# Half-height scores for the first batch, one spread row in place of two, and a new order of the opening

## The chip, the cores and the metric

The kernel runs on one core of one Trainium2 chip. The metric is the device time of one execution in microseconds; the figure for a kernel is the median of its runs. A profiled execution is told beside it, with its own time.

The core has a matrix engine (PE, with its weight loads shown apart as PEld), a vector engine (DVE), an engine for activations and copies (ACT), a general engine (POOL) and an engine that mostly issues transfers (SP). Each takes its instructions in the order of the program. Transfers (DMA) are issued by SP, ACT and POOL into queues that share 16 DMA engines.

## The reference

Eight batches of eight heads; 576 rows of 64 numbers for each head in q, k and v. Keys and values are averaged over groups of 8 rows, so that 72 pooled keys stand for 576. Then a mixing layer over the rows and a two-layer network follow. Cut to what matters:

```python
k_p = k.reshape(B, H, Sp, 8, D).mean(axis=3)          # 72 pooled keys
v_p = v.reshape(B, H, Sp, 8, D).mean(axis=3)
attn = softmax(q @ k_p.T / 8)                          # 576 x 72
x = (attn @ v_p) as (B, 576, 512)                      # heads side by side
tok = einsum('ts,bsd->btd', w_tok, alpha1 * x + beta1)
u = x + lam * tok
out = u + lam * (relu((alpha2 * u + beta2) @ w_ch1) @ w_ch2)
```

## The kernel before

The work is cut into batches (attention) and into blocks of four chunks of 128 rows (mixing and network). The order of all instructions is written out by hand. From the second batch on, attention runs inside the network's work: a list of (due time, step) pairs is sorted and issued. For the first batch there is nothing to hide it in: the code issues it as a plain sequence at the end of the kernel's body, from `keep_warm(13)` to the loop `for j in range(4): mlp_A(0, j, 256, 512)`. That sequence is called the opening here, and it is what the change touches.

The steps of the opening, with the lines of their main instructions:

- `att_F(0, hp)` (L402, copy L409): four transposes of q on PE for a pair of heads, then a copy into `qT`. `att_Frem` (L426, L429): the same for the last 64 rows of all heads, after `cast_rem` (L170).
- `double_k(u)` (L433, and L178, L179 for u = 0) and `att_K(0, u)` (L445, L451): the pooled keys of four heads by 20 small products. The result has the two halves of the row pairs on partitions 0 to 63 and 64 to 127.
- In `att_K`, for the first batch, two copies (L461) put each half into a tile `kpT` whose other half is zero. So `att_S(0, h)` can run each product over all 128 rows: three products for a head (256 columns, 256 columns and 64 columns; L493, L496), and two exponentials on ACT (L498). For later batches `att_K` makes one copy (L457) and `att_S4` runs products over 64 rows each (L513, L520).
- `first_V(0, u)` (L472 over 128 rows, L474 over 32 rows, copy L477): the pooled values of four heads.
- `att_AV(0, h)` (L556, L560, then L562 and L564 on DVE): the weighted values of one head. `att_X` and `rest_X` (L578, L571) multiply by lambda times alpha1, mostly on POOL.
- `spread_lam` (L304, L305) spreads the row lambda over 128 partitions by two passes of a one-row product and a copy on ACT; `spread_al1(half)` (L311, L312) does the same with one half of alpha1 and multiplies by lambda on DVE.
- `setup_wtok` (L329, L332) and `setup_rowsum` (L341, L343) prepare the mixing matrix; `mix_T(0, c)` (L614, then L618, and L624 with `al2_bc` on POOL or DVE) mixes; `mix_uT` (L638, L640) transposes; `mlp_A` (L662, L669) is the first layer of the network.
- `keep_warm(n)` (L605): n products of 512 columns whose result nobody reads.
- `load_al2` (L298, L299): a one-column memset on DVE, and behind it SP's transfer of alpha2, spread over 128 partitions by the transfer itself.

Products write into eight PSUM banks: six taken in turn by `gp`, two by the tag `ch`.

## Time and profile before

| | |
|---|---|
| median of 3 runs | 334.22 us (333.26 to 334.68) |
| the profiled execution | 333.62 us, of which the span of instructions is 331.9 us |
| PE busy | 323.7 us (98%) |
| DVE, ACT, POOL busy | 233.6, 175.7, 95.2 us |
| mean granted PE clock | 0.995 |
| chain that ended last | PE 94%, DMA 2%, DVE 1%, issue 1%, POOL 1% |

How to read it: times inside the execution are counted from the start of the span. The products of PE overlap each other, and their ends are modelled; the spacing of their starts is the firmer number, and it is what is used below. An engine's idle time has a releaser: the instruction whose end let it go on. The chain of waits starts at the last instruction and goes back, at each step to what released it, or to the instruction before it on its engine.

### The profile page before, as it was taken

Reading aid. Unit: us, or ns where it says so; the run is one execution under the profiler, and the core shown is the slowest. Engines: PE = TensorE matmul, PEld = TensorE weight load, DVE = VectorE, ACT = ScalarE, POOL = GpSimd, SP = SyncE. Lnnn points to the kernel's source line nnn. Section 1 sums busy time; section 2 is a strip of 40 time slices with the busy share of each in tenths; the row PEclk is TensorE's granted clock in tenths of the full one; section 3 lists DMA queues with packets and bytes.
Section 4 is the critical chain, followed back from the end, with each engine's and each line's share of the span. In section 5 each row is a group of like instructions: output and inputs, shape, how many; then the busy total and the mean of one; then the engine's idle time right before and its main releaser. Section 6 shows DMA issues by size and latency. Waiting matters only on the chain.

```text
span 331.9 us, 6477 instructions
## 1 busy us (share of the span) xinstructions
PE 323.7 (98%) x2500; PEld 209.6 (63%) x2531; DVE 233.6 (70%) x485; ACT 175.7 (53%) x322; POOL 95.2 (29%) x110
## 2 busy tenths in 40 slices
PE   7999999999999999999999999999999999999995
PEld 3667864455544576656775677558755866586584
DVE  6674289989679969676967796877788783263263
ACT  3584989448422861388128812682268225703710
POOL 8669828401247011800280027102510200000000
PEclk9799999999999999999999999999999999999999
DMA  8999999966895992499449943996340044004003
GB/s 117 191 217 270 270 209 245 206 148 101 152 243 99 219 181 81 80 232 173 147 109 209 173 136 73 209 187 176 65 136 2 0 65 143 2 0 127 1 32 97
DMA packets 66472, 45.81 MB, mean 138 GB/s; under 512 B 34397, under 2 KB 57061, under 8 KB 66442
## 3 DMA queue, kind: packets, MB, share of 16 engines
q1 hardware_dynamic: 52092, 32.67, 43.3%
q0 software_dynamic: 13824, 12.40, 22.9%
q8 instruction: 20, 0.33, 0.4%
q10 hardware_dynamic: 526, 0.34, 0.4%
q14 instruction: 10, 0.08, 0.1%
HBM read 38.30 MB, written 9.44 MB: 144 GB/s over the span
## 4 chain that ended last, share of the span: by engine, by line
PE 94%; DMA 2%; DVE 1%; issue 1%; POOL 1%; ACT 0%; POOLq 0%
PE ps_h L662 38%; PE ps_w L785 26%; PE ps_tok L614 11%; PE ps_ch L682 8%; PE ps_av L556 3%; PE ps_s L513 2%; DMA k<-in_k_dram 2%; PE ps_kp L445 1%; PE ps_sc L493 1%; PE ps_r L520 1%; PE ps_av L560 1%; PE ps_v L472 0%; PE ps_w L329 0%; PE ps_q L402 0%; DVE u_sb L618 0%
## 5 line engine op out<-in xcount | busy, mean ns | idle before, releaser
L662 PE MATMUL ps_h<-u_fm,w 128*128 128x512 bf16 (+2 forms) x588 | 132.6, 368 | 1.3 <-DVE bias_cols L665 0.2
L669 ACT ACTIVATE H<-ps_h,bias_cols 128x512 bf16<-128x512 f32 x144 | 98.2, 688 | 56.5 <-PE ps_h L662 55.5
L662 PEld LDWEIGHTS <-w 128*128 128x128 bf16 x608 | 65.6, 114 | 49.9 <-issue 2.2
L785 PEld LDWEIGHTS <-H 128*128 128x128 bf16 x560 | 53.5, 98 | 10.8 <-DVE u_sb L803 1.2
L622 ACT CAST u_bf<-u_sb 128x512 bf16<-128x512 f32 x32 | 19.8, 618 | 69.9 <-issue 39.9
L785 PE MATMUL ps_w<-w_l,H 128*128 128x256 bf16 x448 | 53.6, 272 | 0.0
L803 DVE TENSOR_TENSOR u_sb<-u_sb,ps_w 128x512 f32<-128x512 f32 x54 | 36.3, 683 | 17.1 <-PE ps_w L785 17.1
L578 POOL TENSOR_TENSOR xs<-x_tm,lamal_bc 128x512 bf16<-128x512 f32 x12 | 15.9, 1328 | 108.7 <-DVE x_tm L564 108.5
L614 PE MATMUL ps_tok<-xs,wtT 128*128 128x512 bf16 (+3 forms) x194 | 44.6, 380 | 0.4
L618 DVE TENSOR_TENSOR u_sb<-x_tm,ps_tok 128x512 f32<-128x512 f32 (+1 forms) x40 | 27.4, 684 | 9.9 <-PE ps_tok L614 9.8
L564 DVE TENSOR_TENSOR x_tm<-ps_av,rec 128x320 f32<-128x320 f32 x64 | 31.5, 492 | 2.6
L542 ACT ACTIVATE ET<-ps_s 72x512 f16<-72x512 f32 x56 | 32.3, 592 | 0.0
L614 PEld LDWEIGHTS <-wtT 128*128 128x128 bf16 (+3 forms) x200 | 17.4, 100 | 16.0 <-issue 1.1
L562 DVE RECIPROCAL rec<-ps_av 128x5 f32<-128x5 f32 x64 | 12.2, 190 | 16.9 <-PE ps_av L560 16.7
L483 DVE TENSOR_TENSOR v_u<-v_u 72x1024 f32<-72x1024 f32 (+1 forms) x24 | 22.7, 948 | 0.2
L785 PE MATMUL ps_w<-w_t,h_s 128*128 128x256 bf16 x168 | 22.6, 272 | 0.0
L682 PEld LDWEIGHTS <-H 128*128 128x128 bf16 x128 | 11.9, 98 | 13.7 <-issue 0.4
L754 DVE TENSOR_TENSOR H<-H,H 128x1024 bf16<-128x1024 bf16 x14 | 9.7, 690 | 14.3 <-ACT H L669 14.2
L185 POOL TENSOR_TENSOR k_raw<-k_raw 128x512 f32<-128x512 f32 x14 | 18.8, 1341 | 0.9 <-PE ps_ch L682 0.7
L785 PEld LDWEIGHTS <-h_s 128*128 128x128 bf16 x168 | 16.4, 98 | 4.1
L187 POOL TENSOR_TENSOR k_bf<-k_raw 128x512 bf16<-128x512 f32 x14 | 18.5, 1319 | 1.1
L754 DVE TENSOR_TENSOR h_s<-H 128x1024 bf16<-128x1024 bf16 x21 | 14.4, 686 | 6.0 <-ACT H L669 5.8
(148 smaller groups left out, 367.6 us busy)
## 6 DMA issues: line engine op xcount, KB each, us to landing
out_dram<-u_sb SPq DMA_DIRECT2D x29, 256.0 KB
k_raw<-in_k_dram SPq DMA_DIRECT2D x12, 512.0 KB
v_u<-in_v_dram SPq DMA_DIRECT2D x12, 512.0 KB
q_bf<-in_q_dram POOLq DMA_DIRECT2D x16, 256.0 KB, 7.3
w<-in_moe_w_ch_dram POOLq DMA_DIRECT2D x6, 512.0 KB, 12.5
out_dram<-u_sb SPq DMA_DIRECT2D x11, 128.0 KB
w<-in_moe_w_ch_dram POOLq DMA_DIRECT2D x1, 1024.0 KB, 15.0
k_raw<-in_k_dram POOLq DMA_DIRECT2D x2, 512.0 KB, 16.8
```

The costliest lines, as they stand in the source:

```text
L483: nc.vector.tensor_tensor(out=out, in0=t[:, :, 0:width], in1=t[:, :, width:2 * width], op=ALU.add)
L542: nc.scalar.activation(out=o, in_=i, func=AF.Exp, bias=0.0, scale=0.125)
L564: nc.vector.tensor_tensor(out=x[:, 1 - odd:6 - odd, dd:dd + D], in0=av[:, :, 0:64], in1=rec.unsqueeze(2).to_broadcast((P, 5, D)), op=ALU.mult)
L614: nc.tensor.matmul(out=ps_tok[p0:p1], lhsT=wtT[0:kk, at, P * c:P * c + p1 - p0], rhs=xs_pool[i][0:kk, sc, :], start=(sc == 0), stop=(sc == 4))
L618: nc.vector.tensor_tensor(out=s["u"][p0:p1, :], in0=x[p0:p1, 1 + c if c < 4 else 5 - 5 * i, :], in1=ps_tok[p0:p1, 0:DM], op=ALU.add)
L622: nc.scalar.copy(out=s["u_bf"], in_=s["u"])
L662: nc.tensor.matmul(out=ps_h[:, t0:t1 + one], lhsT=w1_of(cc, j), rhs=rhs, start=(cc == 0), stop=(cc == 3))
L669: nc.scalar.activation(out=H4[n, j // 4][:, j % 4, :], in_=ps_h, func=AF.Relu, bias=bias_cols[:, j:j + 1], scale=1.0)
L682: nc.tensor.matmul(out=ps, lhsT=H_of(n, j)[:, 128 * m:128 * m + 128], rhs=(w2l if n else w2)[j // 4][:, j % 4, :], start=(j == 0), stop=(j ...
L754: nc.vector.tensor_tensor(out=o, in0=a, in1=b, op=op)
L785: nc.tensor.matmul(out=ps, lhsT=stat(j), rhs=moving(j), stop=(j == 7), start=(first and (pp == 0 or alone) and j == 0), skip_group_check=True)
L803: nc.vector.tensor_tensor(out=o, in0=o, in1=banks[key, "both"], op=ALU.add)
```

## The change

For the first batch `att_K` now makes one copy of the pooled keys, of both halves, as for the later batches; the two `kpT` tiles and their clearing are gone. `att_S` runs its products over 64 rows: one half on partitions 0 to 63, the other on 64 to 127, each with 256 columns, and the 64 columns of the last rows with the half they belong to. The half with those columns is stored behind the other one, and `att_AV` reads the columns in the matching order.

One row is spread in place of two: `lamal_row` multiplies lambda by alpha1 as a single row on DVE, and `spread_lamal` spreads the product to `lamal_bc`. The spread of lambda itself is replaced by a transfer, `load_lam`, issued on SP behind a one-column memset on DVE, with due time 1.5 in the list of block 0. The transfer of alpha1 is issued on ACT's queue right after lambda's, ahead of the last rows of q and k.

The order of the opening is changed, and three further `keep_warm(1)` calls stand in it.

```diff
     load_vector(0, moe_lam)
+    nc.scalar.dma_start(out=vecs[0:1, 2], in_=moe_alpha1.unsqueeze(0))
     load_rem(0)
     load_q_bf(0, 0)
     load_k16(0, 0)
     load_vector(1, moe_beta1, nc.sync)
-    nc.scalar.dma_start(out=vecs[0:1, 2], in_=moe_alpha1.unsqueeze(0))
...
-            t = const.tile([P, 2, 4, SPG], BF, tag=f"kpT_{i}", name=f"kpT_{i}")
-            nc.vector.memset(t, 0.0)
-            kpT_pool.append(t)
...
-    def spread_lam():
+    def lamal_row():
+        nc.vector.tensor_tensor(out=vecs[0:1, 2], in0=vecs[0:1, 2], in1=vecs[0:1, 0], op=ALU.mult)
+
+    def spread_lamal():
 
         ps = gp("ps_bc")
-        nc.tensor.matmul(out=ps, lhsT=ones_row, rhs=vecs[0:1, 0])
-        nc.scalar.copy(out=lam_bc, in_=ps)
-
-    def spread_al1(half):
-
-        ps = gp("ps_bc")[:, 0:256]
-        cols = slice(256 * half, 256 * half + 256)
-        nc.tensor.matmul(out=ps, lhsT=ones_row, rhs=vecs[0:1, 2, cols])
-        nc.vector.tensor_tensor(out=lamal_bc[:, cols], in0=lam_bc[:, cols], in1=ps, op=ALU.mult)
+        nc.tensor.matmul(out=ps, lhsT=ones_row, rhs=vecs[0:1, 2])
+        nc.scalar.copy(out=lamal_bc, in_=ps)
+
+    def load_lam(behind):
+        behind.memset(lam_bc[:, 0:1], 0.0)
+        nc.sync.dma_start(out=lam_bc, in_=moe_lam.unsqueeze(0).to_broadcast((P, DM)))
...
-        if b:
-            copy(out=kp_pool[u], in_=kp)
-            return
-        for a in range(2):
-            rows = slice(64 * a, 64 * a + 64)
-            (copy or (nc.scalar.copy, nc.vector.tensor_copy)[a])(
-                out=kpT_pool[u][rows, a], in_=kp[rows])
+        copy(out=kp_pool[u], in_=kp)
...
         for half in range(2):
-            n0, n = 256 * half, 256 + 64 * half
+            own = half == hh
+            n0, n = 256 * own, 256 + 64 * own
+            rows = slice(64 * half, 64 * half + 64)
             ps_sc = gp("ps_sc")
-            nc.tensor.matmul(out=ps_sc[0:SPG, 0:256], lhsT=kpT_pool[u][:, half, h % 4, :],
-                             rhs=st["qT"][u][:, 2 * (h % 4):2 * (h % 4) + 2, :])
-            if half:
-                nc.tensor.matmul(out=ps_sc[0:SPG, 256:320], lhsT=kpT_pool[u][:, hh, h % 4, :],
-                                 rhs=st["rem_qT"][:, :, h // 2::4].rearrange("p c i -> p i c"))
+            nc.tensor.matmul(out=ps_sc[0:SPG, 0:256], lhsT=kp_pool[u][rows, h % 4, :],
+                             rhs=st["qT"][u][rows, 2 * (h % 4):2 * (h % 4) + 2, :])
+            if own:
+                nc.tensor.matmul(out=ps_sc[0:SPG, 256:320], lhsT=kp_pool[u][rows, h % 4, :],
+                                 rhs=st["rem_qT"][rows, :, h // 2::4].rearrange("p c i -> p i c"))
...
-            m0 = 256 * (c % 2) + 128 * (c // 2)
+            m0 = 256 * (c % 2 if b else c % 2 == h % 2) + 128 * (c // 2)
...
     cast_rem(0, nc.vector)
-    more_constants()
     keep_warm(1)
     att_Frem(0, nc.scalar.copy)
     keep_warm(1)
-    spread_lam()
+    lamal_row()
+    spread_lamal()
     double_k(0)
-    att_K(0, 0, None)
-    spread_al1(0)
-    bias_row(0)
+    att_K(0, 0, nc.vector.tensor_copy)
     att_S(0, 0)
     att_S(0, 1)
+    more_constants()
+    bias_row(0)
+    double_k(1)
     first_V(0, 0)
     att_S(0, 2)
-    double_k(1)
     att_AV(0, 0)
+    att_K(0, 1, nc.scalar.copy)
     att_S(0, 3)
+    att_F(0, 2, nc.vector.tensor_copy)
+    att_F(0, 3)
     att_AV(0, 1)
-    att_K(0, 1, nc.scalar.copy)
-    att_F(0, 2, nc.vector.tensor_copy)
-    late_copy = att_F(0, 3, None)
+    att_X(0, 0, 2, nc.gpsimd, False)
+    att_S(0, 4)
     att_AV(0, 2)
-    att_X(0, 0, 2, nc.gpsimd, False)
+    keep_warm(1)
+    att_S(0, 5)
+    first_V(0, 1)
     att_AV(0, 3)
     att_X(0, 2, 4, nc.gpsimd, False)
     rest_X(0, 0, 4, nc.gpsimd)
-    att_S(0, 4)
-    late_copy(nc.scalar.copy)
-    first_V(0, 1)
+    att_S(0, 6)
+    att_AV(0, 4)
     load_al2(nc.vector)
-    att_S(0, 5)
-    att_AV(0, 4)
-    att_S(0, 6)
-    spread_al1(1)
+    keep_warm(1)
+    att_S(0, 7)
     att_AV(0, 5)
     att_X(0, 4, 6, nc.gpsimd, False)
-    att_S(0, 7)
+    keep_warm(1)
     setup_wtok(0, nc.scalar.copy)
     att_AV(0, 6)
...
         if n == 0:
+            todo.append((1.5, lambda: load_lam(nc.vector)))
             todo.append((6.2, lambda: setup_rowsum(4)))
```

More of the change, by code (lines that the diff above doesn't have):

```diff
@@ L255 @@
     load_wtok()
-    vp1_pool, kpT_pool, kp_pool, ET_pool = [], [], [], []
+    vp1_pool, kp_pool, ET_pool = [], [], []
     for i in range(4):
```

## The prediction

> **What bounds the kernel now.** I read the page first, then the chain of waits of the opening, the windows by clock, and the timelines.

> ```profile
> PE 323.7 (98%) x2500; PEld 209.6 (63%) x2531; DVE 233.6 (70%) x485; ACT 175.7 (53%) x322; POOL 95.2 (29%) x110
> PEclk9799999999999999999999999999999999999999
> ```

> PE is busy all along, so what shortens or lengthens PE's order moves the end. One slice has a clock of 0.7. The windows (length, then PE, PEld, DVE, ACT, POOL busy, clock, DMA share, GB/s) show why:

> ```profile
> 7.54:10.95 3.41, 3.18 (x29) 1.52 (x28) 1.48 (x7) 2.05 (x6) 3.09 (x6) 1.00 1.46 185
> 10.95:14.37 3.42, 3.42 (x22) 2.29 (x22) 1.79 (x6) 1.92 (x7) 1.85 (x3) 0.50 1.32 190
> 33.00:332.00 299.00, 293.64 (x2228) 190.09 (x2254) 213.06 (x416) 157.17 (x278) 70.20 (x73) 1.00 0.62 131
> ```

> From 10.95 to 14.37 the clock is 0.50. Behind 33 us PE works 293.6 of 299 us and the change leaves its order as it is: a shift reached at 33 us goes through to the end. So I have to find that shift. The chain of waits (start, length, what):

> ```profile
> 9.87 0.40 ACT kpT L461
> ...
> 10.29 0.47 DVE kpT L461
> ...
> 10.81 0.33 PE ps_sc L493
> ...
> 18.50 0.62 PE ps_bc L311 x2
> ...
> 25.34 0.70 DVE u_sb L618
> ...
> 26.06 0.69 DVE u_bf L624
> ```

> Two copies of pooled k in a row hold PE; the second spread of alpha1 stands on the path; at the end of the opening DVE and POOL take over from PE. Batch 1 already runs half-height scores (timeline of PE: start, length, x count):

> ```profile
> 39.43 0.59 PE L662 MATMUL ps_h<-u_fm,w 128*128 128x512 bf16 x2
> 39.95 0.30 PE L513 MATMUL ps_s<-qT,kp 64*72 64x256 bf16 x2
> 40.09 0.24 PE L520 MATMUL ps_r<-rem_qT,kp 64*72 64x64 bf16 x2
> 40.16 0.39 PE L513 MATMUL ps_s<-qT,kp 64*72 64x256 bf16 x4
> 40.39 0.24 PE L520 MATMUL ps_r<-rem_qT,kp 64*72 64x64 bf16 x2
> 40.46 0.28 PE L513 MATMUL ps_s<-qT,kp 64*72 64x256 bf16 x2
> 40.67 0.29 PE L445 MATMUL ps_kp<-pool_main,k_bf 128*128 128x64 bf16 x4
> ```

> Four products of 256 columns take 0.23 us (40.16 to 40.39): a pair costs 0.115, as one of 128 rows does (0.109). But the last pair holds PE 0.21 us until the full-height L445, 0.10 more, and at the entry L662's last product (39.65 + 0.216 = 39.86) leaves 0.09. So each change of height costs about 0.095 us (0.135 at half clock, by L472 to L474 at 12.14 to 12.49 against 0.213).

> **The price of the scores.** Before, a head costs 0.109 + 0.109 + 0.075 = 0.29 us at full clock. After, an even head's own half comes first: 0.136, then its 64 columns beside the other half, 0.11: 0.25; an odd head 0.136 + 0.073 = 0.21. Heads 0 and 1 stand together and share two changes of height; the other six stand alone between full-height products, and each pays 0.19 more: 0.44 or 0.40 against 0.29. The half-height scores are thus a gain for one pair and a loss of 0.1 to 0.15 us for each lone head. [...]

> **The walk.** I set all steps of the opening in the new order, engine by engine, with durations of the rows and landings of the trace. The same walk of the old order puts `mix_T`'s first product at 22.73; the trace has 22.68.

> - Copies: one DVE copy of 128x288 (L457: 0.46) from 9.87 replaces 0.40 + 0.47. Scores begin at 10.37, not 10.81 (the first half product of head 0 aside), heads 0 and 1 end by 10.90 with the change out: `first_V` 0.64 us earlier than its 11.54.
> - `first_V` (1.46 at half clock), head 2: `att_AV(0,0)` at 12.95 against 13.64: 0.69.
> - `att_K(0,1)` moves into the half clock: 20 products take 0.97 us in place of 0.57; head 3 follows at 14.33 and `att_F(0,2)` is at 14.72 against 15.15: 0.43 left.
> - Head 4 waits for DVE's copy of that q: 14.94 + 0.2 + 0.42 = 15.6 against 16.05: 0.43.
> - From there to `setup_wtok(0)`: second spread gone, -0.72 with its changes of height; three `keep_warm`, +0.65; lone heads 4 to 7, +0.4; the wait for `vp` (17.60 to 17.87), -0.27; two `att_AV` that stood ahead of head 4, +0.30. That is +0.36 on the trace; the walk, in part because it has the old order 0.13 late there (19.65 against 19.52), gives +0.06. So 0.07 to 0.37 is left. Behind it both walks agree step by step; I take 0.37, since the walk hits `mix_T` within 0.05, and keep 0.07 for the range.

> Hidden edits: the spread of lambda times alpha1 needs `lamal_row` (0.68, a one-row product like L284's) on DVE at 7.03, so it runs 7.76 to 8.83 where L304 ran 7.70 to 8.82, still ahead of k's landing at 8.88; without that cover each 0.1 costs 0.1. `more_constants` (0.67) and `bias_row` (0.68) go behind the copy into DVE's free time from 10.33; behind them `double_k(1)` waits for k's second load (landed 11.94) until 12.17, and `first_V`'s copy needs DVE at 12.42: 0.25 of cover. POOL issues `load_k` 1.1 earlier and has its last product for `mix_T` at 22.05, 0.3 before it is needed; `load_w1(1)` behind it goes from 21.93 to 22.5 and is used at 37. The `kpT` clearing (2 x 0.30) stood in idle DVE time. `load_lam`: memset at about 31, where DVE idles 2.9 us; SP has nothing to do from 24.6 to 37.6 but the copy of `wtT`, which is used behind 60. Its 256 KB push POOL's loads back by 0.76 us (128 packets of 0.095 us on 16 engines, as alpha2's); v lands at 40.29 (28.69 + 11.6) and is used at 41.42, lambda at 47.5. Nothing, then; past that cover up to 0.76.

> **Two unknown landings.** Alpha2's memset now stands behind `att_AV(0,4)`'s work on DVE: 19.34, not 17.76.

> ```profile
> 17.86 0.36 SPq L299 DMA_DIRECT2D al_bc<-in_moe_alpha_dram  x1
> 1.97 0.62 ACTq L148 DMA_DIRECT2D rem_raw<-in_q_dram  x1
> ```

> In the trace its packets start only at 21.3 and its parts land from 22.66 to 24.02. POOL needs it at 24.38 in the new order. From below: the start was set by POOL's w1 packets (0.175 us each until 21.3), and an issue at 19.4 still makes that turn: nothing. From above: 6.2 us after the issue again, 25.6, and the shift becomes +0.32. It decides from 25.0 on. I take the lower, as 21.3 is where those packets thin out. [...]

> Alpha1 (0.52 of issue time) goes ahead of the last q rows on ACT's queue; they landed at 6.79, and DVE's cast waited for them (6.89). From below nothing: issued by 2.60, their packets start at 5.05, so a place in line may set that. From above: between the two loads on that queue 0.70 us of issue made 1.55 of landing (6.79, 8.34), so 1.15. `att_Frem`, `lamal_row`, the spread and `att_K` are queued behind: by the walk a landing at 7.3 makes the shift -0.03, at 7.95 +0.46. I take nothing, by the gap from 2.60 to 5.05.

> **Sum.** -0.37 on the execution of 333.62 us (span 331.9 and 1.7 around it); the median of the runs is 334.22, 0.6 above, so 333.85.

> **Rivals.**
> 1. Alpha2 late: POOL's and DVE's L624 wait. For it: the 6.2 us. Against: the turn. +0.32, to 0.66 with q late as well: 334.6.
> 2. Last q rows late, alone: +0.1 to 0.5: 334.5.
> 3. Slower: q's last rows so late (past about 7.3) that `att_Frem` and a `keep_warm` slide over 7.54. By spacings of starts PE did 2.3 us of work in 4.13 to 7.54 and the clock stayed; 2.0 in 7.54 to 10.95, and it halved. Without these steps the first holds 2.06. Then the clock halves at 7.54 and, if it stays so for two stretches, the walk gives +1.2 to +2.0: 335.8. Against: one such stretch only moves the half clock, +0.0 to 0.4.
> 4. Faster: by the walk, changes of height that cost nothing give -1.3, and a clock that does not halve -1.1: 332.9. Against: the rows above; PE does no more in 7.54 to 10.95 than before (1.8 of 2.0).
> 5. The halves do not run side by side: four odd heads at 0.109, +0.44, 334.3. L513's pairs speak against it.

> **How the numbers follow.** A measurement of this kernel can tell about 0.5% (1.67 us) from no change. Forecast 0.28; rival 1 0.13; rival 2 with 5 0.11; rival 3 0.14 (0.11 over the bound); rival 4 0.12 (0.07 over it with the runs' spread of 0.7); what the walk does not see, further off, 0.12 faster and 0.10 slower. So faster 0.19, same 0.60, slower 0.21. The range takes in rivals 1, 2, 5, most of 3 and 4 with the spread: 332.3 to 336.0.

> **What would show it.** L461 gone and one L457-like copy of 0.46; first L493 near 10.4; lone heads 0.40 to 0.44 from start to next full-height start; `mix_T` at 22.3; L624 on POOL at 24.4 (later: rival 1); the cast of q at 6.9 (later: 2 or 3); half clock in one stretch. The forecast is wrong if the clock is half for none or two, or if PE at 33 us is off by more than 0.5.

## The result, and the profile after

The changed kernel is slower: 338.12 us (median of 7 runs, 334.01 to 339.83) against 332.62 us (331.98 to 334.68, 7 runs: the three of the table above and four more), a ratio of 1.0112 [1.0072, 1.0153]. The ratio comes from the runs compared and not from the two medians, which lie 1.7% apart. The forecast was 333.85 us and no change.

Stretches at half clock come in some executions of a kernel and not in others, so beside a median stands in how many runs at least one came. Before: 22 of 98 runs (all that were timed beside the experiments); changed: 11 of 13 (with e1 below). Without any, the kernel before takes 332.6 us (median of 76) and the changed one 334.0 (2 runs); with them the changed one takes 338.1 (median of nine; two more, at 339.7 and 339.8, had a fifth stretch). So there are two losses: 1.4 us at full clock, and 4.1 us from a clock that is mostly half for four stretches.

The profiled execution of the changed kernel (334.01 us, span 332.3) happened to have no half clock. The first experiment ran the changed kernel again, and its profiled execution (337.66 us, span 336.0) is the usual case. From the pages, first the changed kernel's execution without half clock:

```profile
PE 322.6 (97%) x2499; PEld 207.6 (62%) x2530; DVE 234.8 (71%) x483; ACT 175.0 (53%) x320; POOL 95.9 (29%) x110
PEclk9999999999999999999999999999999999999999
```

and the usual one, in which PE is busy 6.4 us longer, with a clock of 0.7 and 0.5 in the second and third slice:

```profile
PE 329.0 (98%) x2530; PEld 210.8 (63%) x2530; DVE 232.8 (69%) x483; ACT 175.1 (52%) x320; POOL 95.8 (29%) x110
PEclk9759999999999999999999999999999999999999
```

The windows of the execution without half clock (length, then PE, PEld, DVE, ACT and POOL busy, clock, DMA share, GB/s):

```profile
9.13:12.55 3.42, 2.68 (x36) 1.53 (x35) 2.19 (x8) 2.04 (x6) 2.84 (x5) 1.00 1.36 175
12.55:15.96 3.41, 3.11 (x55) 2.33 (x56) 2.39 (x8) 2.85 (x9) 1.69 (x3) 1.00 1.17 208
33.00:332.00 299.00, 293.56 (x2224) 189.72 (x2251) 214.16 (x416) 156.95 (x278) 70.30 (x73) 1.00 0.62 132
```

Behind 33 us PE works 293.56 of 299 us, as before (293.64): the loss is in the opening. The windows of the usual execution:

```profile
8.52:11.93 3.41, 2.86 (x33) 1.64 (x34) 1.84 (x9) 1.36 (x5) 3.35 (x5) 1.00 1.41 177
11.93:15.35 3.42, 3.33 (x40) 2.42 (x40) 1.60 (x6) 2.34 (x8) 1.52 (x2) 0.50 1.24 209
15.35:18.76 3.41, 3.41 (x26) 1.94 (x24) 1.76 (x5) 2.04 (x6) 1.26 (x1) 0.50 1.10 207
18.76:22.17 3.41, 3.41 (x28) 1.73 (x28) 2.20 (x8) 1.41 (x4) 1.73 (x2) 0.50 1.17 205
22.17:25.59 3.42, 3.42 (x31) 2.59 (x29) 1.81 (x7) 1.38 (x2) 2.63 (x4) 0.50 1.30 283
```

Four stretches in a row are at 0.50, and in the one ahead of them PE is busier (2.86 us) than in the 9.13 to 12.55 of the first execution (2.68), which was not followed by a fall. How that can be is the main question below.

The timeline of the changed kernel, execution without half clock (start, length, engine, line):

```profile
7.37 0.32 DVE L170 CAST rem_q<-rem_raw 128x256 bf16<-128x256 f32 x1 [0.87 <-DMA rem_raw<-in_q_dram]
7.61 0.67 DVE L299 TENSOR_TENSOR vecs<-vecs 1x512 f32<-1x512 f32 x1
8.33 1.12 PE L304 MATMUL ps_bc<-vecs,ones_row 1*128 1x512 f32 x2
9.39 0.64 PE L442 MATMUL ps_kp<-pool_main,k 128*128 128x64 bf16 x16
10.15 0.46 DVE L453 CAST kp<-ps_kp 128x288 bf16<-128x288 f32 x1 [1.40 <-PE ps_kp L448]
10.67 0.30 PE L486 MATMUL ps_sc<-qT,kp 64*72 64x256 bf16 x2 [0.55 <-DVE kp L453]
10.81 0.34 PE L486 MATMUL ps_sc<-qT,kp 64*72 64x256 bf16 x2
```

The cast of q's last rows waits for their transfer until 7.37 (before: 6.89). `lamal_row` (L299) follows it on DVE, the spread (L304) follows that, and `att_K` (L442) starts 1.06 us behind the spread's start, though k's first load had landed at 7.76. The two copies of pooled k are one (L453), and heads 0 and 1 run as pairs of halves.

Starts of the same steps, in us. e7 is the kernel before plus one late transfer (see there); its execution had no half clock, so it is the fair partner of "after".

| step | before | e7 | after | after, usual (e1) |
|---|---|---|---|---|
| cast of q's last rows | 6.89 | 6.85 | 7.37 | 7.57 |
| the one-row spread ahead of `att_K` | 7.70 | 7.73 | 8.33 | 8.51 |
| `att_K(0,0)` | 8.93 | 8.78 | 9.39 | 9.56 |
| first score | 10.39 | 10.07 | 10.67 | 10.84 |
| `first_V(0,0)` | 11.54 | 11.00 | 11.09 | 11.26 |
| `setup_wtok(0)` | 19.52 | 18.00 | 18.44 | 21.88 |
| `mix_T(0,0)` | 22.68 | 21.16 | 21.74 | 26.82 |
| first `mlp_A` | 28.12 | 26.61 | 27.94 | 32.26 |

### The profile page after: what moved, and what is told of

It is laid out like the page before. It is cut to its first block, busy times and chain, and to the rows that moved or that the text cites. A ratio compares the mean times of both kernels' runs of the same rounds, so it can differ in the third digit from the quotient of the medians.

```text
span 332.3 us, 6473 instructions
## 1 busy us (share of the span) xinstructions
PE 322.6 (97%) x2499; PEld 207.6 (62%) x2530; DVE 234.8 (71%) x483; ACT 175.0 (53%) x320; POOL 95.9 (29%) x110
## 4 chain that ended last, share of the span: by engine, by line
PE 94%; DVE 2%; DMA 1%; ACTq 1%; issue 1%; ACT 0%
PE ps_h L655 38%; PE ps_w L778 26%; PE ps_tok L607 12%; PE ps_ch L675 8%; PE ps_av L549 3%; PE ps_s L506 2%; DMA b2row<-in_moe_beta_dram 1%; PE ps_kp L442 1%; PE ps_r L513 1%; PE ps_av L553 1%; DVE u_bf L617 0%; PE ps_warm L598 0%; ACTq L148 0%; PE ps_q L399 0%; PE ps_sc L486 0%
## 5 line engine op out<-in xcount | busy, mean ns | idle before, releaser
L662 ACT ACTIVATE H<-ps_h,bias_cols 128x512 bf16<-128x512 f32 x144 | 98.2, 689 | 55.5 <-PE ps_h L655 54.5
L615 ACT CAST u_bf<-u_sb 128x512 bf16<-128x512 f32 x32 | 19.8, 618 | 71.1 <-issue 39.6
L474 DVE TENSOR_TENSOR v_u<-v_u 72x1024 f32<-72x1024 f32 (+1 forms) x24 | 22.7, 947 | 0.2
```

Of the source, the lines that this page charges most:

```text
L474: nc.vector.tensor_tensor(out=out, in0=t[:, :, 0:width], in1=t[:, :, width:2 * width], op=ALU.add)
L615: nc.scalar.copy(out=s["u_bf"], in_=s["u"])
L662: nc.scalar.activation(out=H4[n, j // 4][:, j % 4, :], in_=ps_h, func=AF.Relu, bias=bias_cols[:, j:j + 1], scale=1.0)
```

## The experiments

Times are medians; ratios are to the kernel before on the same chip, from the runs compared and not from the medians. A run counts as one with half clock when its mean clock shows at least one such stretch. The letters in the expectations are the theories' names.

**The change and its undoing, part by part (e1 to e4).** e1 is the changed kernel again. e2 gives it back the full-height scores and their two copies of k. e3 is the kernel before with only the half-height scores and the single copy. e4 is the changed kernel with alpha1's load in its old place:

```diff
-    nc.scalar.dma_start(out=vecs[0:1, 2], in_=moe_alpha1.unsqueeze(0))
     load_rem(0)
...
     load_vector(1, moe_beta1, nc.sync)
+    nc.scalar.dma_start(out=vecs[0:1, 2], in_=moe_alpha1.unsqueeze(0))
```

Expected of e1: 

> The changed kernel once more, for a profile of an execution with a low mean clock. Its profiled execution had a clock of 1.000 and took 334.0 us; four others had 0.979 and took about 338.1, that is 336.4 x (1 - 0.979) x 2 = 14 us at half clock, four stretches of 3.41 us. All theories expect most runs at 337.5 to 338.5 with a mean clock near 0.98. Theory H (half-height products count as less work for the clock): the half clock lies where the scores are, 10 to 20 us, and goes on as long as lone heads do. Theory G (the gap that the late last rows of q leave before the product of k): it begins at 7 to 10 us, and the first window with the gap decides. Theory O (order: short waits between the opening's steps, whatever the height).

Expected of e2: 

> The changed kernel with the scores of the first batch over 128 rows again, from the two half-empty copies of pooled k (ACT and DVE for the first four heads, ACT twice for the others); loads, one spread row and order as in the changed kernel. Theory H: mean clock back to 0.995 or more, 333 to 334.5 us. Theories G and O: clock stays near 0.98, 337.5 to 339.

Expected of e3: 

> The kernel before with only the half-height scores and the single copy of pooled k; order, loads and the two spreads as before. Theory H: mean clock 0.98, 337 to 339 us. Theories G and O: clock 0.995, 333 to 335 (a lone head costs 0.1 us more, the copy 0.4 less).

Expected of e4: 

> The changed kernel with the load of alpha1 back in its old place on ACT's queue, behind the last rows of q and k. The cast of q's last rows goes back from 7.37 to about 6.9 us; the one-row product on DVE waits for alpha1 (landed about 7.7) and the spread then runs at 8.4 to 9.5 as in the changed kernel. Theory G: the gap of 0.97 us ahead of the transposes of q's last rows moves behind a keep_warm and is shorter, fewer stretches at half clock, 334 to 336 us. Theories H and O: clock near 0.98, about 338.

| | median us | ratio | runs with half clock | median without |
|---|---|---|---|---|
| e1, changed | 338.03 | 1.0112 [1.0063, 1.0161] | 5 of 6, mostly four stretches | 334.0 (1 run) |
| e2, full-height scores | 336.71 | 1.0085 [1.0051, 1.0118] | 8 of 12, one to three | 334.2 |
| e3, half-height scores alone | 334.19 | 1.0019 [0.9989, 1.0049] | 7 of 12, one to four | 332.6 |
| e4, alpha1 late | 335.70 | 1.0079 [1.0044, 1.0114] | 6 of 12, mostly four | 334.2 |

The heights cost nothing at full clock (e3: 332.6, as before), and their undoing does not mend the change (e2). They seem to make half clock more frequent (7 of 12 runs, against 7 of 29 of the kernel before on the same chip and 22 of 98 on all). In e4 q's last rows are early again (cast at 6.5), but then `lamal_row` waits for alpha1 until 7.97, the spread starts at 8.71 and `att_K` at 9.76, as late as before the undoing: whichever row lands last holds the spread. No theory of the first round holds alone; what goes with the loss is the clock.

**What the clock goes by (e5, e6, e9).** A reading of the first six profiles suggested a rule: take a stretch of 3.41 us of the clock's own (its records in the trace of before begin at 4.13 and change at 10.95 and 14.37, behind 6.83 and 3.41 us), sum each product's streaming time weighted by its rows over 128, and divide by 3.41. The streaming times are estimates from the trace of before. Two products of 256 columns (L472) start 0.213 us apart at a clock of 0.50 and 0.109 at 1.00; so products of 512 are put at 0.213 at 1.00, where they start 0.216 apart in a row, and at 0.427 at 0.50. Each fp32 product of the spread is put at 0.427 at 1.00: with 512 columns (L304: 0.692 and 0.587 us) it lasts 0.213 longer than with 256 (L311: 0.478 and 0.374); the two of 512 start 0.53 apart. In the usual execution's stretch 8.52 to 11.93 the spread streams for 0.85 us but counts 0.01, as it has one row; `att_K` counts 0.46, the scores of 64 rows 0.24, `first_V` 0.46: 1.17 in all, a share of 0.34. A share under some 0.37 would let the clock fall. Three kernels test that rows count. e5 adds idle products where PE waits, and e6 the same with 32 rows:

```diff
+    fill(2)          # 512 columns, 128 rows (e6: warm[0:32, 0:P], warm[0:32])
     att_Frem(0, nc.scalar.copy)
...
     att_K(0, 0, nc.vector.tensor_copy)
+    fill(2)
     att_S(0, 0)
...
     att_S(0, 2)
+    fill(1)
     att_AV(0, 0)
```

Expected of e5: 

> The changed kernel with five more idle products of 128 rows and 512 columns (0.21 us each) where PE stood idle in its trace: two ahead of att_Frem, two between att_K(0,0) and the scores, one ahead of the first att_AV. W (the clock falls when the streaming time of a 3.41 us stretch, each product weighted by its rows over 128, is under about 0.37 of it): the poorest stretch rises from 0.34-0.38 to 0.46 or more, no half-clock stretch in the opening, nearly every run between 333.5 and 335.0. B (PE's plain busy share decides): the same here, as the busy share rises too. T (something else than PE's load, such as the moment of loads): four half-clock stretches in most runs as in the change, 337.5 to 338.5.

Expected of e6: 

> The same five products at the same places, of the same 512 columns and so of the same time, but contracting only 32 rows. W: they add a quarter as much (0.03 of a stretch), the clock falls as often as in the change: four half-clock stretches in more than half of the runs, median 337 or more. B: rows don't matter, so no half-clock stretch, 333.5 to 335.0 as with 128 rows.

e5: 333.52 us, 1.0027 [0.9998, 1.0055], half clock in 2 of 12 runs. e6: 337.95 us, 1.0153 [1.0118, 1.0189], half clock in 4 of 4. In e6's timeline and windows:

```profile
10.32 0.60 PE L604 MATMUL ps_warm<-early 32*128 32x512 f16 x2
8.26:11.68 3.42, 3.32 (x35) 1.61 (x34) 1.85 (x10) 1.29 (x3) 3.42 (x6) 1.00 1.49 193
11.68:15.09 3.41, 3.41 (x36) 1.98 (x35) 2.16 (x5) 1.70 (x7) 1.05 (x2) 0.50 1.28 214
```

PE is busy 3.32 of 3.42 us (2.41 us of it streaming, halves side by side counted once), and the clock falls all the same; the weighted share is 0.35. In e5's stretch of the same place PE is busy less, the weighted share is 0.44, and the clock stays:

```profile
7.84:11.25 3.41, 3.21 (x35) 1.40 (x33) 2.00 (x8) 1.43 (x3) 3.39 (x6) 1.00 1.44 182
11.25:14.67 3.42, 3.08 (x48) 1.88 (x43) 2.26 (x7) 2.41 (x8) 1.29 (x3) 1.00 1.32 203
```

e9 goes further and adds no product: the spread itself contracts 128 rows of which only the first is not zero.

```diff
-        nc.tensor.matmul(out=ps, lhsT=ones_row, rhs=vecs[0:1, 2])
+        nc.tensor.matmul(out=ps, lhsT=first_row, rhs=lamal)   # rows 1 to 127: zeros
```

Expected: 

> The changed kernel, but the one spread (1.12 us of fp32 products) contracts 128 rows, of which only the first isn't zero, in place of one row: the same values, place and columns; three clearings more on DVE where it idles. W: this stretch gains up to 1.07/3.41 = 0.31 of weighted share, so it no longer falls under 0.37; no half-clock stretch in nearly all runs, 333.6 to 334.6, though not one step is taken out or moved. B (rows don't matter): as the change, 337.5 to 338.5, four half-clock stretches in most runs.

333.81 us, 1.0020 [1.0001, 1.0040], half clock in none of 12 runs, although here q's last rows came later than in any profile above (cast at 8.0). The spread's line and the stretch it stands in (e9):

```profile
9.07 1.13 PE L310 MATMUL ps_bc<-lamal,first_row 128*128 128x512 f32 x2
8.21:11.62 3.41, 2.50 (x31) 1.44 (x31) 2.15 (x9) 0.96 (x2) 2.82 (x6) 1.00 1.49 194
11.62:15.04 3.42, 3.06 (x53) 2.14 (x50) 2.34 (x8) 2.77 (x9) 1.99 (x3) 1.00 1.30 215
```

The spread takes as long as with one row (1.12), PE is busy least of the three kernels (2.50), and the clock holds, at a weighted share of 0.55. e10 and e11 below spread over 128 rows too and have half clock in none of 24 runs, while e12, with the one-row spread on the same chip, has it in 7 of 12. That rows count is shown, and 4.3 us of the loss are gone with one operand.

The eighteen traces also settle two rival counts. Unweighted streaming does not separate the stretches: the clock fell behind shares of 0.46 to 0.76 and stayed behind 0.46 and up. Weighting by the columns of the weights as well does not either: it fell behind 0.18 to 0.36 and stayed behind 0.27 (the changed kernel's 9.13 to 12.55). Rows alone do.

**Why four stretches (e22).** Over the openings of all profiles the clock fell behind shares of 0.22 to 0.36 and stayed from 0.38 on; at half clock it stayed half behind shares up to 0.74 and rose behind 0.72 to 1.0. So it would need about twice as much to rise as to stay. e22 puts four 128-row products into the stretch behind the fall. (In it, and in its control e19, the transposes of the later blocks are on PE in place of DMA; that lengthens the kernels by some 29 us and brings two half-clock stretches at 88 to 100 us (e19's mean clock is 0.991 over 361.0 us), so only the opening is read.)

```diff
     att_S(0, 2)
+    fill(1)
     att_AV(0, 0)
+    fill(1)
     att_K(0, 1, nc.scalar.copy)
     att_S(0, 3)
+    fill(1)
     att_F(0, 2, nc.vector.tensor_copy)
+    fill(1)
     att_F(0, 3)
```

Expected of e19: 

> Control for e20 to e22: the kernel before, with the transposes of q and u in the later blocks done on TensorE and copied by ScalarE in place of by DMA; the opening (to 33 us) is untouched. Opening as before: scores at 10.1, mix_T at 21.2, the first mlp_A at 26.6 at full clock, half-clock stretches in about a quarter of the runs. Some 3 to 8 us longer in all, by 14 chunks of 4 transposes and three batches of q on PE.

Expected of e22: 

> The changed kernel (later transposes on TensorE as in e19) with four idle 128-row products of 0.21 us (0.43 at half clock) between the scores of head 2 and att_F(0,3), about 12.5 to 15.5 us, behind the stretch whose poverty lets the clock fall. W with a higher bound for going back (about 0.75 of a half-clock stretch): it falls as often as in the change, but the stretch behind it has 0.85 or more and it comes back after one or two stretches: in runs with half clock 1 to 2 half-clock stretches, and 2 to 3.5 us above e19's full-clock runs. F (a fixed length of four stretches): four stretches in most runs, 5.5 to 6.5 us above e19's.

e22: 366.91 us, e19: 362.37. The opening's windows in e22:

```profile
7.80:11.21 3.41, 2.78 (x32) 1.42 (x33) 1.97 (x9) 1.19 (x4) 3.41 (x6) 1.00 1.41 177
11.21:14.62 3.41, 3.41 (x24) 1.89 (x25) 2.09 (x6) 1.91 (x6) 1.26 (x2) 0.50 1.33 210
14.62:18.04 3.42, 3.42 (x37) 2.46 (x34) 0.67 (x3) 1.47 (x4) 0.75 (x1) 0.50 1.07 205
```

Two stretches, not four, and by the mean clocks so in all five runs (4.1 to 4.5 half-clock stretches each; in the profile two of them are later, as in e19). A fixed length is out, as it is by the profiles of e2 (two stretches) and of e3, e8 and the kernel before (one). The weighted shares are 0.32, 0.71 and 0.82: the rise came behind the second, and the 0.85 expected of the stretch behind the fall was not reached. The forecast of 2 to 3.5 us above e19 missed (4.5); the cost of the added products at half clock and what the later blocks add were not told apart. The control missed too: 29 us longer, not 3 to 8.

**What is lost at full clock (e7, e8, e10, e11, e12).** e7 adds to the kernel before only the change's `load_lam` and its place in block 0.

```diff
+            todo.append((1.5, lambda: load_lam(nc.vector)))
             todo.append((6.2, lambda: setup_rowsum(4)))
```

Expected: 

> The kernel before plus the change's load of lambda alone (memset on DVE and 256 KB on SP's queue in block 0; it writes the same values over lambda's spread). L (the 1.3 us that the change loses even at full clock come from this transfer's push on v, k and w loads): 334.0 to 334.5 in runs without a half-clock stretch. O (they come from the new order of the opening): 332.4 to 333.1, as before. The opening is as before in both, so most runs have no half-clock stretch.

332.51 us, 0.9995 [0.9974, 1.0016]: the transfer is free, as the forecast had it.

e8 is the kernel before with the change's lambda part alone, in the old order and with full-height scores.

```diff
-    spread_lam()
+    lamal_row()
+    spread_lamal()
...
-    spread_al1(0)
...
-    spread_al1(1)
```

Expected: 

> The kernel before with the change's lambda part alone: alpha1 loaded ahead of q's last rows, lamal_row on DVE and one spread in place of spread_lam and the two spread_al1, lambda loaded in block 0; order and full-height scores as before. O: the second spread_al1 (0.62 and its wait) is gone from PE's path at 18 us, so 332.2 to 333.0 at full clock, with half-clock stretches in about a quarter of the runs as before. L or a late q: 333.5 to 334.5 at full clock. W: without the second spread's weightless 0.6 us the stretches behind 16 us get richer, the one at 8 us stays as poor as before (0.22 to 0.35).

335.78 us, 1.0100 [1.0062, 1.0139], half clock in 5 of 6 runs. Both theories expected 332.2 to 334.5 at full clock; the one such run took 334.78, so both missed. By the medians this part alone gives 3.2 of the 5.5 us. In its profile the cast of q's last rows is at 7.64, `lamal_row` at 8.59 behind `more_constants`, the spread at 9.26 and `att_K` at 10.31, 1.5 later than in e7; the stretch 8.86 to 12.27 has a share of 0.22.

e12 is the kernel before with alpha1's load moved and nothing else.

Expected: 

> The kernel before with alpha1's load alone moved ahead of q's last rows on ACT's queue. Q (this is what makes q's last rows late): their cast starts at 7.4 to 7.7 in place of 6.5 to 7.2; the spread of lambda slides from 7.7 to 8.5, att_K to 9.4 or later; 0.3 to 0.8 us more at full clock, and more runs with half-clock stretches than before's quarter: median 333.3 to 335. R (their landing scatters by itself): 6.5 to 7.2 and 332.4 to 333 as before.

334.63 us, 1.0049 [1.0018, 1.0081], half clock in 7 of 12 runs, 332.9 without. Its timeline:

```profile
7.42 0.29 DVE L170 CAST rem_q<-rem_raw 128x256 bf16<-128x256 f32 x1 [0.92 <-DMA rem_raw<-in_q_dram]
8.20 1.12 PE L304 MATMUL ps_bc<-vecs,ones_row 1*128 1x512 f32 x2
9.25 0.64 PE L445 MATMUL ps_kp<-pool_main,k 128*128 128x64 bf16 x16
```

A load of 2 KB put ahead of q's last rows makes them late: cast at 7.36 to 8.5 in the thirteen profiles of kernels that have it there (in e10 and e11 a clearing on DVE stands right ahead of the cast), 6.5 to 7.2 in the five that do not. `att_K` again starts 1.05 behind the spread; k had landed at 8.05.

e10 is e9 with alpha2's load issued earlier, and e11 is e10 with the spread cut in two halves of 256 columns, behind `att_K(0,0)` and ahead of the first `att_AV`.

```diff
-    spread_lamal()
     double_k(0)
     att_K(0, 0, nc.vector.tensor_copy)
+    spread_lamal(0)
     att_S(0, 0)
...
     att_S(0, 2)
+    spread_lamal(1)
     att_AV(0, 0)
```

Expected of e10: 

> As e9, with alpha2's load issued some 3 us earlier (behind the scores of head 4 in place of att_AV of head 4). A (alpha2's landing holds u_bf back at full clock, 24.6 against 24.0): first product of mix_T to first of uT 3.8 us as in the kernel before, not 4.3, and 0.3 to 0.6 us less than e9. N (it moves other transfers as much as it gains): same time as e9 within 0.2.

Expected of e11: 

> As e10, with the spread cut into two halves of 256 columns (0.55 us each), one behind att_K(0,0) where PE waits for the copy of pooled k, one ahead of the first att_AV. S (the spread stands between q's late last rows and att_K): pooled k's first product at 8.7 to 8.9 in place of 9.4 to 9.7 and 0.3 to 0.6 us less than e10, as the second half fits its gap only in part. K (k's own landing holds att_K): no earlier than 9.3, and the same time as e10 or up to 0.5 more.

e10: 333.45 us, 1.0007 [0.9985, 1.0028]; 0.36 under e9, which supports the late alpha2 but is near what runs differ by. e9's own profile had `mix_T` so late that alpha2 held POOL without holding PE (3.8 us from `mix_T` to `mix_uT` in e9 and e10), so its rows don't tell. e11: 333.20 us, 0.9997 [0.9974, 1.0019]. In e11:

```profile
8.24 0.94 PE L449 MATMUL ps_kp<-pool_main,k 128*128 128x64 bf16 x16
9.12 0.68 PE L311 MATMUL ps_bc<-lamal,first_row 128*128 128x256 f32 x2
```

`att_K` starts at 8.24, 0.14 behind k's landing (8.10) and over 1 us earlier than in the changed kernel: the spread was what held it. The gain to the end is only 0.25 us; in this profile `wt_bf` landed at 18.16 and `setup_wtok(0)` waited for it until 18.21.

**The old order with e11's spread (e20, e21).** e20 has full-height scores, e21 half-height ones; both are read against e19.

Expected of e20: 

> e19's order and full-height scores, with the changed kernel's early alpha1 and lambda's late load, and e11's two half spreads of 128 rows (behind att_K(0,0) and ahead of the first att_AV); the DVE constants behind the first scores. O (the new order loses the rest): scores start at 9.8 to 10.1, first_V some 0.4 later than in e11 (two copies of k), from first_V to setup_wtok(0) 6.5 to 7.0 where e11 took 8.0 and the kernel before 7.0, so mix_T at 20.5 to 21.2 unless wtok's landing (16.8 to 18.5) holds it; 0.1 to 0.8 us under e19 at full clock, no half-clock stretches. H (the lone heads' half heights lose it): the same here, but e21 is slower than this by 0.5 or more.

Expected of e21: 

> As e20, with half-height scores from the one copy of pooled k. O: first_V 0.4 us earlier than in e20, six lone heads at 0.1 to 0.15 more each give 0.6 to 0.9 back; within 0.4 of e20. H: 0.5 or more above e20, and mix_T at 21.6 as in e11.

361.99 and 362.52 us against e19's 362.37: no difference that these six runs each can tell, and no version that beats the kernel before. From `att_K` to `first_V` e20 takes 2.51 us and e21 2.00, so the one copy gives 0.5; from `first_V` to `setup_wtok(0)` they take 6.50 and 6.83, so the lone half-height heads give 0.33 of it back. The last 0.6 us between e11 (333.2) and the runs of the kernel before without half clock (332.6) are not traced to a step: landings move by more than that from one execution to another (`wt_bf` at 16.8 to 19.8).

## Why the prediction was wrong

**The clock: the step that failed, and worth 4.1 us.** The walk kept the half-clock stretch of the one trace, "in one stretch", and judged its likelihood by PE's work counted alike. What went with the falls is work weighted by rows (up to 0.36 of a stretch fell, from 0.38 on stayed): the 2.0 us that the prediction counted in the stretch 7.54 to 10.95 of the trace before weigh 0.22 of it, its 2.3 in the one ahead 0.71. The change puts the one-row spread into the middle of the stretch that has least else in it, makes the first scores half-height, and starts `att_K` behind both. Rival 3 named the right event (q's last rows late, the clock falls, more than one stretch), but at a chance of 0.14, by the wrong count and at 335.8; four stretches came. Its argument against, "one such stretch only moves the half clock", assumed that the clock comes back after one. The half clock of the trace before was also not the kernel's usual case (22 of 98 runs), so the walk compared with a slow opening: without it `mix_T` stands at 21.16 (e7), not 22.68. That the profiled 334.01 us lies near the forecast of 333.85 is therefore luck: it has no half-clock stretch where the walk had one, and loses at other steps about what that saves.

**The hidden edits: the spread was not hidden, 0.6 us.** "Still ahead of k's landing at 8.88": that landing is 7.76 in the changed kernel's trace, 7.8 to 8.6 in all but one profile with the early alpha1, and 8.3 to 9.1 in those without. So 8.88 was one draw, and the cover was smaller with alpha1 early; the spread, later by q's 0.5, became what `att_K` waits for (9.39 against 8.78). The text's own price, "without that cover each 0.1 costs 0.1", is what happened.

**Q's last rows.** "I take nothing" was wrong: 0.5 us in the trace, inside its bounds of 0 to 1.15. The reasoning from the gap between issue and first packet (2.60 to 5.05) did not hold; the place in the queue mattered, as e12 shows.

**Alpha2.** Rival 1's event is in the trace of the changed kernel. In the lines of the timeline, first after, then e7, POOL's and DVE's products for `mix_uT`:

```profile
24.76 1.25 POOL L617 TENSOR_TENSOR u_bf<-u_sb,al_bc 128x512 bf16<-128x512 f32 x1 [2.03 <-DMA al_bc<-in_moe_alpha_dram]
25.11 1.45 DVE L617 TENSOR_TENSOR u_bf<-u_sb,al_bc 128x512 bf16<-128x512 f32 x1
```

```profile
23.24 1.26 POOL L628 TENSOR_TENSOR u_bf<-u_sb,al_bc 128x512 bf16<-128x512 f32 x1 [2.04 <-DVE u_sb L622]
24.54 0.69 DVE L628 TENSOR_TENSOR u_bf<-u_sb,al_bc 128x512 bf16<-128x512 f32 x1
```

It landed at 24.61, 6.07 us behind its issue at 18.54: the upper estimate of 6.2, not the turn that was taken. With the opening at full clock POOL had been idle since 22.73. From `mix_T` to the first `mlp_A` it takes 6.20 us against 5.45 in e7; how much of these 0.75 an earlier alpha2 gives back is only supported by e10's 0.36. In the execution with half clock (e1) `mix_T` is later and alpha2 is in time.

**The price of the scores was right.** Forecast 0.40 for an odd lone head. In the timeline of the changed kernel, head 5 between an idle product and `first_V`:

```profile
15.19 0.38 PE L598 MATMUL ps_warm<-early 128*128 128x512 f16 x1
15.50 0.30 PE L486 MATMUL ps_sc<-qT,kp 64*72 64x256 bf16 x2
15.81 0.63 PE L463 MATMUL ps_v<-v,pool_v 128*72 128x256 f16 x4
```

With the 0.216 us that lie between the starts of two such products, the idle one streams until 15.19 + 0.216 = 15.41, and `first_V` starts at 15.81: head 5 takes 0.40. The halves do run side by side: in the timeline above heads 0 and 1 take 0.42 us from 10.67 to `first_V` at 11.09, with their last rows and the change of height, where four products of 256 columns one behind the other (0.109 each, L472 of before) would take 0.44 without either. So rival 5 is out. Rival 4's free changes of height are out with it.

**The walk's checkpoints.** Measured against e7 and counted from `att_K`, `first_V` comes 0.52 earlier (forecast 0.64 with the half clock), `setup_wtok(0)` 0.17 earlier, `mix_T` 0.03 earlier, where 0.07 to 0.37 was left. So the reordering's gain came and was given back inside the opening, as forecast in kind; the 0.6 of the late `att_K` and the 0.75 behind `mix_T`, where alpha2 is late, are the 1.33 by which the first `mlp_A` is later.

## What to carry to other kernels

Before moving small things in an opening, look where the clock stands near its edge: count PE's work by rows, as the count that fits these traces does: there a one-row spread is next to nothing (0.01 us for 0.85) and a product of half height half, and the clock fell behind shares up to 0.36 and stayed from 0.38 on. A spread of one row did not bring the clock down (e9) when it contracted 128 rows with zeros in the rest; its time was the same (1.13 us against 1.12). And a cover that is a landing time must be read from several executions, above all when the change moves a load in the queues.
